# RetNet attention and a PReLU feed-forward layer on one core: a planner that counts changes between kinds of matmul, and a last unit ordered by accumulator

## The chip, the cores and the metric

The kernel runs on one core of a Trainium2 chip. The metric is device time in microseconds (us). The engines are TensorE (PE in the profile; PEld are its weight loads), VectorE (DVE), ScalarE (ACT), GpSimd (POOL) and SyncE (SP), which issues nearly all DMAs. Each engine works through its own queue in order and waits on semaphores for the others.

## The reference

```python
# q, k, v: (8 batches, 8 heads, 576, 64), fp32
scores = 1/sqrt(64) * q @ k^T
Dmat   = where(rel >= 0, gamma[h] ** rel, 0)        # gamma[h] = 1 - 2**(-5-h)
x      = ((scores * Dmat) @ v)  -> (4608 tokens, 512)
h      = x @ w_in                                   # 512 x 2048
g      = max(h, 0) + alpha * min(h, 0)
out    = g @ w_out                                  # 2048 x 512
```

## The kernel before, in words

**The feed-forward layer** is cut into 18 blocks of 256 tokens and 8 units of 256 hidden columns. A *cell* is one block with one unit. A *visit* is one block with several units in a row (`order`): first 17 visits with units 0 to 3, then one with all eight, then 17 visits with units 4 to 7. The four PSUM banks `pso` gather a visit's output and are emptied after its last cell (`evacuate`, L1116): one operation takes in the second accumulator `p1` (VectorE at L1123, or a ScalarE copy at L1127 in first visits), a second one on VectorE combines it with the first accumulator `p0` (L1128), and a DMA writes the result. This is done for each half `m` of the block's tokens.

**Products of pieces.** Plain fp32 products on TensorE are slow. So every operand is split into pieces in a type with fewer mantissa bits (`fp32r`), and three products of pieces replace one fp32 product: two go into one accumulator, and the product of the *differences* (piece 2 of each operand) goes into another. `unit` (L1042) does so for `x @ w_in`: 12 matmuls for each half `f` of the unit's columns (L1057) into the bank `psh[f]`, then two ScalarE and two VectorE operations for each (the last is L1071, and it frees the bank). `split_g` makes the pieces of g on ScalarE and GpSimd. `second` (L1093) does `g @ w_out`: for each m six matmuls at L1105, two cells later (`LAG`). The first 8 cells are done in plain fp32 (`unit_plain` L992, `second_plain` L1023) while the weights are being read and split.

**Attention.** Heads go in 32 pairs. The first eight pairs (batches 0 and 1) are done in the first 110 us by other routines, in fp32. For the other 24, `joint(n)` (L840) gives TensorE three groups of small fp32 matmuls (`GROUPS`): `v0` and `v1`, the values of the pair before (L808, 36 matmuls in two halves, into `psh[0]` and `psh[1]`), and `x` with `su`, the scores and the state sums of this pair (L860, L867, L870, into `psh[1]` and two banks `psa`). The masks (L888) and the state recurrence (L902) follow on VectorE. I call one `joint` an attention step. The banks `psh` are shared with `unit`, so a step's first half must wait for the unit's L1071.

**What sets the order.** The kernel lists operations with `do(engine, cost, function, reads, writes, ...)` and then calls `plan()` (L238). A first pass, backwards, gives each operation a due time. A second pass builds each engine's queue: among the operations whose inputs are done it takes the earliest possible start `t0`, keeps those that could start within `SLACK` after it (0.14 us on TensorE, 0.05 elsewhere), and of these picks the one with the earliest due time. An operation whose `kind` is not that of the one before it on its engine counts as later by `SWITCH` (0.12 on TensorE). The kind is the engine, save for the group with `su`, whose kind is `"half"`. TensorE may run ahead in the program by up to 150 operations. The chip then runs the queues in this order: planned times are no times on the chip, only the order is.

```python
return t + SWITCH.get(op.eng, 0.0) * (kinds[op.eng] != op.kind)
...
t, op = min((x for x in c if x[0] <= t0 + SLACK.get(e, 0.05)),
            key=lambda x: (due[x[1].n], x[1].n))
```

Of the kernel before, what the change touches and what calls it, by code (L numbers as in the profile page):

```python
# [21 lines left out]
def kernel(  # L22
# [315 lines left out]
    BACKLOG, HOLD = 2.0, 30.0  # L338
    LAG, HOLD_X = 2, 100.0
    GROUPS = (("v0",), ("v1",), ("x", "su"))  # L340
    SLACK, SWITCH = {"PE": 0.14}, {"PE": 0.12}
    BEGIN = {"PE": 5.0, "ACT": 0.5, "DVE": 8.2, "POOL": 5.8, "SP": 0.5}


# [488 lines left out]
    def on_pe(parts, groups):  # L833
        for some in groups:
            do("PE", sum(parts[x][0] for x in some), lambda some=some: [parts[x][1]() for x in some],
               [key for x in some for key in parts[x][2]],
               [key for x in some for key in parts[x][3]],
               kind="half" if "su" in some else None)

    def joint(n):  # L840
        pv = [Gen(psh[m]) for m in range(2)]
        parts = {}
        if n - 1 in mts:
            (parts["v0"], parts["v1"]), rest = values(n - 1, pv)
        if n == len(pairs):
            on_pe(parts, [["v0"], ["v1"]])
            rest()
            return
        c = pairs[n][1]
        kT, qT = turned[n]  # L850
        kn, vn = loaded[n][2:]

        ss, uu = (Gen(x) for x in psa)

        def chunks(x):
            return x.get().rearrange("p (j s) -> p j s", s=C)

        def f():
            for h2 in range(2):
                nc.tensor.matmul(pv[1].get()[half(h2), 7 * C:], kT.get()[half(h2), chunk(NJ - 1)],  # L860
                                 qT.get()[half(h2), chunk(NJ - 1)], start=True, stop=True)
        parts["x"] = 0.067, f, [(kT, 0), (qT, 0)], [(pv[1], "x")]

        def f():
            for j in range(NJ - 1):
                for h2 in range(2):
                    nc.tensor.matmul(chunks(ss)[half(h2), j], kT.get()[half(h2), chunk(j)],  # L867
                                     qT.get()[half(h2), chunk(j)], start=True, stop=True,
                                     skip_group_check=True)
                    nc.tensor.matmul(chunks(uu)[half(h2), j], kn.get()[half(1 - h2), j],  # L870
                                     vns[n % 2][half(1 - h2), h2, j], start=True, stop=True,
                                     skip_group_check=True)
        parts["su"] = (1.05, f, [(kT, 0), (qT, 0), (kn, 0), (kn, 1), (vn, "v", 0), (vn, "v", 1)],
                       [(ss, 0), (uu, 0), (uu, 1)])
        on_pe(parts, [some for some in ([x for x in group if x in parts] for group in GROUPS)
                      if some])
        if n - 1 in mts:
            rest()
            if n + 1 < len(pairs):
                load_v(n + 1)  # L880
        mt = mts[n] = Gen(ats)
        for h2 in range(2):
            to = lambda h2=h2: mt.get()[half(h2), h2].rearrange("p j s -> p (j s)")
            dma(to, lambda h2=h2: qT.get()[half(h2)], S * D * 4, [(qT, 0)], [(mt, "q", h2)])

        def masked(h2, j, fro):
            x, h = half(h2), 2 * c + h2
            nc.vector.scalar_tensor_tensor(  # L888
                out=mt.get()[half(1 - h2), h2, j], in0=fro[x], scalar=pf[x, 1, h:h + 1],
                in1=mask[x, None, :].to_broadcast([C, fro.shape[1], C]), op0=ALU.mult,  # L890
                op1=ALU.mult)
        for h2 in range(2):
            do("DVE", 0.69, lambda h2=h2: masked(h2, slice(0, NJ - 1), chunks(ss)), [(ss, 0)],
               [(mt, "s", h2)])
        for h2 in range(2):
            do("DVE", 0.285, lambda h2=h2: masked(h2, slice(NJ - 1, NJ), chunks(pv[1])[:, 7:]),
               [(pv[1], "x")], [(mt, "x", h2)])
        su = Gen(sus)
        g1, g2 = gch[:, 0, c:c + 1], gch[:, 1, c:c + 1]
        do("ACT", 0.37, lambda: nc.scalar.copy(su.get()[:, 0::2], chunks(uu)[:, 0::2]), [(uu, 0)],  # L900
           [(su, "e")])
        do("DVE", 0.45, lambda: nc.vector.scalar_tensor_tensor(  # L902
            out=chunks(uu)[:, 1::2], in0=su.get()[:, 0::2], scalar=g1, in1=chunks(uu)[:, 1::2],
            op0=ALU.mult, op1=ALU.add), [(su, "e")], [(uu, 1)])
        do("ACT", 0.22, lambda: nc.scalar.copy(su.get()[:, 1], chunks(uu)[:, 1]), [(uu, 1)],
           [(su, 1)])
        for j in range(3, NJ - 1, 2):
            do("DVE", 0.285, lambda j=j: nc.vector.scalar_tensor_tensor(
                out=su.get()[:, j], in0=su.get()[:, j - 2], scalar=g2, in1=chunks(uu)[:, j],
                op0=ALU.mult, op1=ALU.add), [(su, j - 2), (uu, 1)], [(su, j)])  # L910
        do("DVE", 0.42, lambda: nc.vector.scalar_tensor_tensor(
            out=su.get()[:, 2::2], in0=su.get()[:, 1:NJ - 3:2], scalar=g1,
            in1=chunks(uu)[:, 2::2], op0=ALU.mult, op1=ALU.add),
            [(su, 1), (su, 3), (su, 5), (uu, 0)], [(su, "e")])
        for h2 in range(2):
            to = lambda h2=h2: vns[n % 2][half(h2), h2, 1:]
            keys = [(su, x) for x in ("e", 1, 3, 5, 7)]
            dma(to, lambda h2=h2: su.get()[half(h2)], (S - C) * D * 4, keys, [(vn, "s", h2)])
# [123 lines left out]
    def unit(cell):  # L1042
        vis, u = cell["vis"], cell["u"]
        x = vis["x"]
        ga = Gen(gas[cell["n"] % 2])
        for f in range(2):
            ph = Gen(psh[f])

            def at(b, ph=ph):
                return ph.get()[:, b * TB:(b + 1) * TB]  # L1050

            def mm(f=f, at=at):
                for n, (b, l) in enumerate(((0, 0), (1, 2), (0, 1))):
                    for cc in range(NCC):
                        w = w_piece(u, cc // 2, l)
                        c0 = (cc % 2 * 2 + f) * P
                        nc.tensor.matmul(at(b), w[:, c0:c0 + P],  # L1057
                                         piece(x.get()[:, l, cc]), start=(n == 0 and cc == 0),
                                         stop=(n > 0 and cc == NCC - 1), skip_group_check=True)
            do("PE", 1.43, mm, [(x, l, n) for l in range(3) for n in range(2)] +  # L1060
               [w_at[u, i][l] for i in range(2) for l in range(3)], [(ph, 0), (ph, 1)])
            fc = 2 * u + f
            g = lambda f=f: ga.get()[:, f]
            do("ACT", 0.36, lambda g=g, at=at: nc.scalar.copy(g(), at(1)), [(ph, 1)], [(ga, f)])  # L1064
            do("DVE", 0.42, lambda g=g, at=at: nc.vector.scalar_tensor_tensor(  # L1065
                out=g(), in0=at(0), scalar=ONE, in1=g(), op0=ALU.mult, op1=ALU.subtract),
                [(ph, 0)], [(ga, f)])
            do("ACT", 0.39, lambda g=g, at=at: nc.scalar.activation(at(1), g(), ACTF.Relu,  # L1068
                                                                    scale=-1.0),
               [(ga, f)], [(ph, 1)])  # L1070
            do("DVE", 0.48, lambda g=g, at=at, fc=fc: nc.vector.scalar_tensor_tensor(  # L1071
                out=g(), in0=at(1), scalar=malpha[:, fc:fc + 1], in1=g(), op0=ALU.mult,
                op1=ALU.add), [(ph, 1), (cst, "a")], [(ga, f)])
        cell["ga"] = ga
# [18 lines left out]
    def second(cell):  # L1093
# [5 lines left out]
                dma(lambda: vis["o"].get(), lambda: o_kept[vis["kb"]], P * 4096,  # L1099
                    [(okm[vis["kb"]], 0), (okm[vis["kb"]], 1)], [(vis["o"], 0), (vis["o"], 1)])  # L1100
        for m in range(2):
            def mm(m=m, a=list(acc)):
                for f in range(2):
                    for b, l in ((0, 0), (0, 1), (1, 2)):
                        nc.tensor.matmul(a[2 * m + b].get(),  # L1105
                                         piece(g.get()[:, l, f, m * P:(m + 1) * P]),
                                         w_piece(u, 2 + f, l),
                                         start=(cell["first"] and f == 0 and l != 1),
                                         stop=(cell["last"] and f == 1 and l > 0))
            do("PE", 1.375, mm, [(g, l) for l in range(3)] +  # L1110
               [w_at[u, i][l] for i in (2, 3) for l in range(3)],
               [(acc[2 * m], 0), (acc[2 * m + 1], 0)])
            if cell["last"]:
                evacuate(vis, m)

# [248 lines left out]
```

## Time and profile before

| | |
|---|---|
| Median of three runs | 954.3 us (952.51 to 955.4) |
| The profiled execution, its own time | 958.57 us |
| Its span, first to last instruction | 956.5 us |
| Mean granted TensorE clock | 0.994 of full |
| TensorE busy | 930.8 us, 97% of the span |
| VectorE, ScalarE, GpSimd busy | 554.1, 573.8, 576.8 us |
| L1057 / L1105, share of the chain that ended last | 40% / 39% |

The span is what the profiler recorded between the first and the last instruction; the execution's own time has some 2 us more around it. A matmul's shown duration contains its way through the array, which overlaps the next one: the difference of two starts is what it costs in a row. "PE psh L808 <- DVE ga L1071" reads: TensorE's instruction of line 808, which writes psh, waited for VectorE's instruction of line 1071.

### The profile page before, as it was taken

To read this page: it belongs to the slowest core of one execution; us is meant where nothing else is said; L and a number is where in the kernel's file an instruction comes from. 1 tells how busy PE (TensorE), PEld (TensorE's weight loads), DVE (VectorE), ACT (ScalarE), POOL (GpSimd) and SP (SyncE) were. 2 spreads that over 40 slices of the span, in tenths; PEclk is the share of its full clock that TensorE was granted. 3 is DMA by queue.
4 is the path that set the end of the run, shared out by engine and by line. 5 is a ranking of instruction groups with operands and counts; after the bars stand their busy time and mean duration, and the time that the engine had idled before them with its cause. 6 is when DMAs were issued, how large, how long until landed. Compare 5 with 4: busy or idle time off the path is not lost.

```text
span 956.5 us, 22974 instructions
## 1 busy us (share of the span) xinstructions
PE 930.8 (97%) x9009; PEld 820.8 (86%) x9009; DVE 554.1 (58%) x1180; ACT 573.8 (60%) x1285; POOL 576.8 (60%) x473
## 2 busy tenths in 40 slices
PE   4899999999999999999999999999999999999998
PEld 4666689888988898888999999999999999999996
DVE  5668566665766676766665754544444554444444
ACT  3446556657667666657876775555555555555542
POOL 3557765748865668745775565555555555555543
PEclk9899999999999999999999999999999999999999
DMA  8867587777877877785434411122222111121212
GB/s 213 203 178 149 134 182 170 151 173 166 186 181 179 199 178 171 209 174 147 155 121 144 156 54 45 67 78 78 86 88 70 67 67 66 66 67 68 66 45 66
DMA packets 235532, 121.05 MB, mean 127 GB/s; under 512 B 203408, under 2 KB 203424, under 8 KB 235424
## 3 DMA queue, kind: packets, MB, share of 16 engines
q1 hardware_dynamic: 233312, 119.05, 47.4%
q8 instruction: 71, 1.16, 0.5%
q10 hardware_dynamic: 2112, 0.53, 0.3%
q14 instruction: 37, 0.30, 0.1%
HBM read 74.19 MB, written 31.98 MB: 111 GB/s over the span
## 4 chain that ended last, share of the span: by engine, by line
PE 91%; DVE 2%; POOL 2%; ACT 2%; issue 1%; DMA 1%; ACTq 0%; POOLq 0%; DVEq 0%
PE psh L1057 40%; PE pso L1105 39%; PE psh L808 3%; PE pso L1023 2%; PE psh L992 2%; PE psa L870 2%; DMA w<-in_q_dram 1%; PE psh L860 1%; PE psa L867 1%; POOL w L732 1%; ACT x L571 1%; DVE psa L679 0%; POOL w L423 0%; ACT w L669 0%; POOL lx L975 0%
## 5 line engine op out<-in xcount | busy, mean ns | idle before, releaser
L1057 PEld LDWEIGHTS psh<-lx,w 128*128 128x128 f32 x2832 | 356.3, 191 | 11.6 <-DVE ga L1071 0.6
L1057 PE MATMUL psh<-lx,w 128*128 128x256 f32 x2832 | 364.2, 284 | 0.0
L1105 PE MATMUL pso<-w,g 128*128 128x512 f32 x1416 | 350.0, 393 | 1.4 <-DVE o L1128 1.2
L1084 POOL TENSOR_TENSOR g<-ga,g 128x512 fp32r<-128x512 f32 x136 | 175.8, 1293 | 243.4 <-ACT g L1080 217.8
L1105 PEld LDWEIGHTS pso<-w,g 128*128 128x128 f32 x1416 | 256.5, 189 | 50.0 <-DVE o L1128 1.4
L1065 DVE SCALAR_TENSOR_TENSOR ga<-psh,ga 128x256 f32<-128x256 f32 x272 | 115.0, 423 | 192.8 <-ACT ga L1064 189.3
L1087 POOL TENSOR_TENSOR g<-g 128x512 fp32r<-128x512 f32 x136 | 176.0, 1294 | 11.7 <-ACT g L1082 1.5
L1064 ACT COPY ga<-psh 128x256 f32<-128x256 f32 x272 | 101.3, 373 | 134.7 <-PE psh L1057 118.4
L1071 DVE SCALAR_TENSOR_TENSOR ga<-psh,malpha,ga 128x256 f32<-128x256 f32 x272 | 130.7, 481 | 69.5 <-ACT psh L1068 68.6
L1068 ACT ACTIVATE psh<-ga 128x256 f32<-128x256 f32 x272 | 105.6, 388 | 82.1 <-DVE ga L1065 81.8
L1080 ACT ACTIVATE g<-ga 128x512 fp32r<-128x512 f32 x136 | 85.7, 630 | 55.9 <-DVE ga L1071 52.1
L975 POOL TENSOR_TENSOR lx<-lx 128x512 fp32r<-128x512 f32 x66 | 84.7, 1295 | 44.4 <-DVE lx L965 36.2
L1082 ACT ACTIVATE g<-ga 128x512 fp32r<-128x512 f32 x136 | 84.4, 620 | 0.0
L888 DVE SCALAR_TENSOR_TENSOR at<-psa,pf,mask 64x512 f32<-64x512 f32 x48 | 36.0, 750 | 31.6 <-PE psa L867 29.0
L958 ACT ACTIVATE lx<-x 128x512 fp32r<-128x512 f32 x66 | 41.2, 627 | 0.0
L808 PEld LDWEIGHTS psh<-at,vn 128*64 128x64 f32 x864 | 27.9, 137 | 10.8 <-issue 6.8
L972 POOL TENSOR_TENSOR lx<-x,lx 128x512 fp32r<-128x512 f32 x24 | 31.0, 1294 | 5.0 <-DVE wa L681 2.1
L693 POOL TENSOR_TENSOR wa<-wa,op 128x512 int32<-128x512 int32 x16 | 21.0, 1311 | 21.5 <-DVE wa L690 11.7
L808 PE MATMUL psh<-at,vn 128*64 128x64 f32 x864 | 32.6, 226 | 1.1 <-DVE ga L1071 1.1
L1123 DVE TENSOR_TENSOR op<-pso,op 128x512 f32<-128x512 f32 x34 | 23.3, 687 | 15.3 <-PE pso L1105 15.3
L965 DVE TENSOR_TENSOR lx<-x,psa 128x512 fp32r<-128x512 f32 x42 | 28.5, 679 | 2.7 <-PE psh L1057 2.1
L827 ACT COPY x<-psh 128x256 f32<-128x256 f32 (+3 forms) x72 | 20.7, 321 | 15.3 <-PE psh L808 11.7
(210 smaller groups left out, 1114.4 us busy)
## 6 DMA issues: line engine op xcount, KB each, us to landing
xk<-x SPq DMA_DIRECT2D x18, 512.0 KB, 4.2
out_dram<-o SPq DMA_DIRECT2D x36, 256.0 KB, 2.3
ok<-o SPq DMA_DIRECT2D x34, 256.0 KB, 3.2
x<-xk SPq DMA_DIRECT2D x17, 512.0 KB, 4.9
op<-ok SPq DMA_DIRECT2D x17, 512.0 KB, 4.0
qx<-in_q_dram SPq DMA_DIRECT2D x96, 72.0 KB, 3.1
kx<-in_k_dram SPq DMA_DIRECT2D x96, 72.0 KB, 2.7
kn<-in_k_dram SPq DMA_DIRECT2D x48, 144.0 KB, 3.2
```

The lines of the kernel that those rows point to most:

```text
L808: nc.tensor.matmul(pv[i].get()[half(h2), (j - js[0]) * C:(j - js[0] + 1) * C], vns[n % 2][:, h2, j], mt.get()[:, h2, j], start=True, stop= ...
L975: do("POOL", 1.29, lambda c=c: nc.gpsimd.tensor_tensor(out=piece(to.get()[:, 2, c]), in0=to.get()[:, 0, c], in1=to.get()[:, 1, c], op=ALU. ...
L1057: nc.tensor.matmul(at(b), w[:, c0:c0 + P], piece(x.get()[:, l, cc]), start=(n == 0 and cc == 0), stop=(n > 0 and cc == NCC - 1), skip_grou ...
L1064: do("ACT", 0.36, lambda g=g, at=at: nc.scalar.copy(g(), at(1)), [(ph, 1)], [(ga, f)])
L1065: do("DVE", 0.42, lambda g=g, at=at: nc.vector.scalar_tensor_tensor(out=g(), in0=at(0), scalar=ONE, in1=g(), op0=ALU.mult, op1=ALU.subtrac ...
L1068: do("ACT", 0.39, lambda g=g, at=at: nc.scalar.activation(at(1), g(), ACTF.Relu, scale=-1.0), [(ga, f)], [(ph, 1)])
L1071: do("DVE", 0.48, lambda g=g, at=at, fc=fc: nc.vector.scalar_tensor_tensor(out=g(), in0=at(1), scalar=malpha[:, fc:fc + 1], in1=g(), op0=A ...
L1080: do("ACT", 0.64, lambda: nc.scalar.mul(piece(to.get()[:, 2]), ga.get(), BELOW), both, [(to, 2)])
L1082: do("ACT", 0.64, lambda: nc.scalar.mul(piece(to.get()[:, 0]), ga.get(), BELOW * 2.0 ** -12), both, [(to, 0)])
L1084: do("POOL", 1.29, lambda: nc.gpsimd.tensor_tensor(out=piece(to.get()[:, 1]), in0=ga.get(), in1=to.get()[:, 2], op=ALU.subtract), both + [ ...
L1087: do("POOL", 1.29, lambda: nc.gpsimd.tensor_tensor(out=piece(to.get()[:, 2]), in0=to.get()[:, 0], in1=to.get()[:, 1], op=ALU.subtract), [( ...
L1105: nc.tensor.matmul(a[2 * m + b].get(), piece(g.get()[:, l, f, m * P:(m + 1) * P]), w_piece(u, 2 + f, l), start=(cell["first"] and f == 0 a ...
```

## The change

Four edits to what the planner is told, and one to the order of matmuls:

- the width `SLACK` of TensorE's choice goes from 0.14 to 0.3, and the price `SWITCH` from 0.12 to 0.1;
- the kinds are drawn anew: products of pieces (`unit`, `second`) have the kind `"pieces"`, all other TensorE work keeps the kind of the engine, and the group with `su` is no longer a kind of its own;
- some costs that the planner reads change: `x` 0.067 to 0.02, `su` 1.05 to 1.09, the masks 0.69 to 0.75, the first step of the recurrence 0.45 to 0.485;
- in a visit's last cell, `second` becomes two operations for each m: first the two products of differences (term `(1, 2)`, into accumulator `2m + 1`), then the other four (into `2m`). In all other cells the six stay one operation in the order of before.

```diff
-    SLACK, SWITCH = {"PE": 0.14}, {"PE": 0.12}
+    SLACK, SWITCH = {"PE": 0.3}, {"PE": 0.1}
...
             do("PE", sum(parts[x][0] for x in some), lambda some=some: [parts[x][1]() for x in some],
                [key for x in some for key in parts[x][2]],
-               [key for x in some for key in parts[x][3]],
-               kind="half" if "su" in some else None)
+               [key for x in some for key in parts[x][3]])
...
-        parts["x"] = 0.067, f, [(kT, 0), (qT, 0)], [(pv[1], "x")]
+        parts["x"] = 0.02, f, [(kT, 0), (qT, 0)], [(pv[1], "x")]
...
-        parts["su"] = (1.05, f, [(kT, 0), (qT, 0), (kn, 0), (kn, 1), (vn, "v", 0), (vn, "v", 1)],
+        parts["su"] = (1.09, f, [(kT, 0), (qT, 0), (kn, 0), (kn, 1), (vn, "v", 0), (vn, "v", 1)],
...
-            do("DVE", 0.69, lambda h2=h2: masked(h2, slice(0, NJ - 1), chunks(ss)), [(ss, 0)],
+            do("DVE", 0.75, lambda h2=h2: masked(h2, slice(0, NJ - 1), chunks(ss)), [(ss, 0)],
...
-        do("DVE", 0.45, lambda: nc.vector.scalar_tensor_tensor(
+        do("DVE", 0.485, lambda: nc.vector.scalar_tensor_tensor(
...
             do("PE", 1.43, mm, [(x, l, n) for l in range(3) for n in range(2)] +
-               [w_at[u, i][l] for i in range(2) for l in range(3)], [(ph, 0), (ph, 1)])
+               [w_at[u, i][l] for i in range(2) for l in range(3)], [(ph, 0), (ph, 1)], kind="pieces")
...
         for m in range(2):
-            def mm(m=m, a=list(acc)):
-                for f in range(2):
-                    for b, l in ((0, 0), (0, 1), (1, 2)):
-                        nc.tensor.matmul(a[2 * m + b].get(),
-                                         piece(g.get()[:, l, f, m * P:(m + 1) * P]),
-                                         w_piece(u, 2 + f, l),
-                                         start=(cell["first"] and f == 0 and l != 1),
-                                         stop=(cell["last"] and f == 1 and l > 0))
-            do("PE", 1.375, mm, [(g, l) for l in range(3)] +
-               [w_at[u, i][l] for i in (2, 3) for l in range(3)],
-               [(acc[2 * m], 0), (acc[2 * m + 1], 0)])
+
+            terms = ((0, 0), (0, 1)), ((1, 2),)
+            for some in reversed(terms) if cell["last"] else (sum(terms, ()),):
+                def mm(m=m, a=list(acc), some=some):
+                    for f in range(2):
+                        for b, l in some:
+                            nc.tensor.matmul(a[2 * m + b].get(),
+                                             piece(g.get()[:, l, f, m * P:(m + 1) * P]),
+                                             w_piece(u, 2 + f, l),
+                                             start=(cell["first"] and f == 0 and l != 1),
+                                             stop=(cell["last"] and f == 1 and l > 0))
+                do("PE", 0.459 * len(some), mm, [(g, l) for _, l in some] +
+                   [w_at[u, i][l] for i in (2, 3) for _, l in some],
+                   [(acc[2 * m + b], 0) for b in sorted({b for b, _ in some})], kind="pieces")
             if cell["last"]:
                 evacuate(vis, m)
```

## The prediction

> **What bounds the kernel now.** I read the page's engine table first, then the stages by window, then who kept TensorE waiting, then TensorE's order of instructions around the attention steps, and last the end of the chain of waits.
>
> The engine table:
>
> ```profile
> PE 930.8 (97%) x9009; PEld 820.8 (86%) x9009; DVE 554.1 (58%) x1180; ACT 573.8 (60%) x1285; POOL 576.8 (60%) x473
> ```
>
> No other engine is above 60%, so the order and the kind of TensorE's matmuls set the time. The stages (length, then busy time and instructions of each engine, granted clock, DMA share, GB/s):
>
> ```profile
> 24.00:110.00 86.00, 79.49 (x1295) 56.92 (x1295) 56.64 (x97) 46.03 (x86) 53.73 (x48) 0.97 0.72 170
> 110.00:455.00 345.00, 342.45 (x4245) 301.19 (x4244) 229.10 (x513) 222.34 (x532) 226.01 (x181) 1.00 0.74 174
> 455.00:945.00 490.00, 490.00 (x3138) 446.98 (x3137) 252.18 (x514) 296.73 (x656) 285.12 (x222) 1.00 0.25 83
> ```
>
> From 455 to 945 us TensorE never stops, and only products of pieces run there: no order of the same matmuls is shorter. From 110 to 455 us the attention steps (fp32 matmuls on 64 rows or columns) are mixed into the products of pieces, with 2.55 us of idle time. From 24 to 110 us all is fp32, with 6.5 us of idle time. TensorE's waits after 110 us (who, for whom: us in total, times, longest):
>
> ```profile
> PE pso L1105 <- DVE o L1128: 1.2, 1, 1.2
> PE psh L808 <- DVE ga L1071: 1.1, 3, 0.6
> PE pso L1105 <- POOL g L1087: 0.3, 1, 0.3
> ```
>
> How the kinds follow each other, on TensorE's timeline: first a stretch of pieces alone, then an attention step cut in two, then one in one piece. (Starts are exact; shown lengths overlap, so a duration is the difference of starts.)
>
> ```profile
> 606.54 2.91 PE L1105 MATMUL pso<-w,g 128*128 128x512 f32 x12
> 609.29 0.40 PE L1057 MATMUL psh<-lx,kx 128*128 128x256 f32 x2
> ...
> 612.16 2.91 PE L1105 MATMUL pso<-w,g 128*128 128x512 f32 x12
> ```
>
> ```profile
> 174.49 1.55 PE L1105 MATMUL pso<-w,g 128*128 128x512 f32 x6
> 175.97 0.80 PE L808 MATMUL psh<-at,vn 128*64 128x64 f32 x20
> 176.70 1.66 PE L1105 MATMUL pso<-w,g 128*128 128x512 f32 x6
> 178.29 0.69 PE L808 MATMUL psh<-at,vn 128*64 128x64 f32 x16
> ...
> 180.10 1.70 PE L1057 MATMUL psh<-lx,w 128*128 128x256 f32 x12
> ```
>
> ```profile
> 392.02 1.27 PE L808 MATMUL psh<-at,vn 128*64 128x64 f32 x36
> ...
> 394.42 2.29 PE L1057 MATMUL psh<-lx,w 128*128 128x256 f32 x17
> ```
>
> Alone, twelve L1105 matmuls take 609.29 - 606.54 = 2.75, so six take 1.375. Six before an attention part take 175.97 - 174.49 = 1.48 (0.105 more); six between two parts take 178.29 - 176.70 = 1.59 (0.215 more). And the attention work itself, 36 of L808 and then scores and state sums, takes 2.40 in one piece (392.02 to 394.42) but 0.73 + 1.81 = 2.54 in two. One cut costs 1.48 + 1.59 + 2.54 = 5.61 against 1.375 + 1.48 + 2.40 = 5.255: **0.355 us a cut**. I counted the cuts along this timeline from 110 to 455 us: nine of the 24 steps are cut (at 133, 176, 190, 218, 235, 291, 361, 376 and 437 us).
>
> The end of the chain (start, us, what):
>
> ```profile
> 944.84 5.91 PE pso L1105 x26
> ...
> 950.77 0.70 DVE op L1123
> ...
> 951.49 0.69 DVE o L1128
> 952.18 0.64 DVE op L1123
> ...
> 952.85 0.69 DVE o L1128
> ```
>
> The last matmul ends at 952.09; then two VectorE operations of 0.69 follow, one after the other, and the output's transfer.
>
> **What the Trainium skill says.** "TensorEngine Tiling (Array Packing)", Key Properties: changing the tiling mode, not just the tile, drains TensorE. The trace agrees: L808 works on 64 columns, L1105 on 128, and each border costs about 0.1 us. "TensorE: Matmul & The Clock Gate", Part 2, step 1: only weight loads are pulled ahead, matmuls stay in program order. The trace agrees: in the one wait of 1.17 us (412.58) no later matmul steps in, so an order planned a little wrong is paid in full. "PSUM — Partial Sum Buffer", Terms: two engines must not be in one bank (and quadrant) at once. The kernel before does as this says: each VectorE read of an accumulator starts after that bank's last product. Products sorted by bank therefore let one bank be read while the other is being filled.
>
> **The change part by part.** Against the profiled execution's own time, 958.57 us (its span is 956.5).
>
> *Last unit's products by bank.* For each visit the two matmuls into the second accumulator come first, then the four into the first one. The same six matmuls (1.375), no extra weight load, no DMA moved. In the middle of the run the subtraction or copy starts four matmuls earlier, 4 x 2.75 / 12 = 0.92, and nothing waits there except once at 412 us. At the end it shows: the first half's subtraction then runs under TensorE; its second operation goes at 950.77; the second half's subtraction follows at about 951.5, its bank being full at 950.74 + 0.46 = 951.2; and the last operation starts at about 952.2 instead of 952.85. Gain 0.65 to 0.71; I take **-0.7**. If the planner orders the last four groups otherwise it is 0: bounds 0 and -0.7.
>
> *Changes of kind counted at 0.1 between pieces and everything else.* Before, 0.12 was counted only around the group of scores and sums, even between it and the L808 work beside it, where the trace shows no cost, and nothing was counted where the 0.1 is really lost. Now, after the first L808 half, a piece product counts as 0.1 later, and with the width of 0.3 the second half is still a candidate when it is ready up to 0.4 later (0.14 before). So I ask when the second half could have started: its bank is free at the end of the L1071 operation of the unit's second half, plus 0.06 (133.35 to 133.41 in the trace). The waits against the end of the first half: 176 us 0.27, 190 us none, 218 us none, 291 us 0.06, 361 us 0.17; at 376 us 0.71 and at 133 us 1.36, too late; 235 and 437 us are of another pattern. Five cuts fall: 5 x 0.355 - 0.27 - 0.06 - 0.17 = 1.28. I take **-1.3**. Bounds: all nine fall without idle time, 9 x 0.355 = -3.2; or the earlier due time, which still decides inside the width, keeps them cut, 0.
>
> *The waits.* 0.31 + 0.27 us at 133 us belong to a cut step, 0.18 and 0.62 to the last two steps, 1.17 to the evacuation at 412 us. A new order moves them all; the two at 133 us are the likeliest to go if that step starts one group later: **-0.6**; bounds -2.55 (all gone) and +1.5 (two more like the largest of before).
>
> *Width 0.3 instead of 0.14.* The planner may leave TensorE idle up to 0.3 for an operation with an earlier due time. At 0.14 the trace shows no such idle time except the five waits, so such near misses are rare. Leaving pieces for an attention part now tolerates 0.3 - 0.1 = 0.2 instead of 0.14: 24 steps x 0.06 = 1.4 at most; among pieces 0.3 instead of 0.14. I take **+0.4**; bounds 0 and +5 (an idle of 0.2 in each of the 24 steps). Between 24 and 110 us all is one kind, so only the width acts: waits of 6.5 us can be shuffled; I take 0, bounds -1.5 and +1.5, a wait like the largest there (1.7) lost or gained.
>
> *Other costs.* 0.69 to 0.75 for the masks (the trace has 750 ns), 0.45 to 0.485 (0.49), 0.067 + 1.05 to 0.02 + 1.09: numbers that only the planner reads, the last pair nearly the same sum. Nothing on the chip, 0; their effect on order lies within the bounds above. Where a gap closes in an attention step the next limit is TensorE's own matmuls.
>
> Sum: -0.7 - 1.3 - 0.6 + 0.4 = **-2.2**, so 956.4 for the profiled execution, 0.23%; on the median of 954.3 this is **952.1**.
>
> **The rivals.** *Nearly all cuts and waits go:* of 3.2 + 2.55 + 0.7 = 6.45 us some 4.5 is gained, 949.8. For it: two cuts fall without idle time and two with next to none. Against it: two lack 0.7 us or more. *Only the end is gained:* the due time decides inside a width three times the price of a change, so the cuts stay, -0.7: 953.6. For it: before, the due time also decided. Against it: a second half that is ready anyway has the earlier due time by its place in the program. *TensorE waits for what is due (the other side):* the wider choice puts idle time before the first L808 part of the steps, where it waits for L1071 and the bank. It costs up to 0.2 each against pieces and 0.3 among them; at 0.25 in each of 24 steps, +6.0 against a gain of 2.6, it is +3.4: 957.7. It decides from about 0.11 us a step on against any gain, and from 0.23 for a slowdown that can be told. Against it: TensorE is at 342.45 of 345 us in this stage with the width of 0.14.
>
> **How the numbers follow.** Main case 0.50, nearly all 0.24, only the end 0.15, waiting 0.11. 0.3% is 2.86 us (the three runs shown spread by as much): faster is under 951.44, slower over 957.16. The main case, with a spread of about 1.5, is under 951.44 in a third, which with 0.95 of the second gives 0.40; slower comes from two thirds of the last, 0.08; same 0.52. The range goes from 948.5 (most of the second case) to 956.2 (all but the waiting case and its early variant).
>
> **What would show it.** Right: fewer L808 groups than steps-plus-nine on TensorE's timeline, six L1105 at 1.59 nearly gone, the last subtraction before TensorE's last end, the stage 455 to 945 us unchanged in length. Wrong: idle time before L808 or L1057 in most steps, or new waits before 110 us; a difference of more than 2 us before 110 us would mean that the width, not the counting, decides the result.

## The result

The changed kernel takes 949.32 us (median) against 954.3 before: the ratio is 0.994, with a 95% interval of 0.9922 to 0.9959. That is 5.0 us or 0.52% by the medians, inside the range and beyond the forecast of 952.1, close to the rival in which nearly all cuts and waits go (949.8). Run a second time beside other kernels it gave 0.9953 (0.9939 to 0.9968).

The engine table of the changed kernel, the line that answers to the first one shown of before:

```profile
PE 924.4 (98%) x9009; PEld 817.5 (86%) x9009; DVE 549.3 (58%) x1180; ACT 572.0 (60%) x1285; POOL 576.6 (61%) x473
```

The same 9009 matmuls, 6.4 us less of busy time. To see where, I cut both traces at three points that mean the same work in both: the first matmul of the first attention step, the first matmul after the last L808 and the end of the last matmul. First the kernel before (length, then busy time and instructions of each engine, clock, DMA share, GB/s):

```profile
0.00:112.19 112.19, 93.46 (x1605) 68.03 (x1605) 71.07 (x154) 54.75 (x99) 65.24 (x72) 0.95 0.73 176
112.19:451.66 339.47, 336.92 (x4214) 296.99 (x4213) 226.53 (x508) 218.66 (x524) 220.56 (x176) 1.00 0.75 176
451.66:952.09 500.43, 500.43 (x3196) 455.81 (x3192) 255.06 (x518) 300.40 (x663) 290.95 (x227) 1.00 0.25 82
```

Then the changed kernel:

```profile
0.00:107.59 107.59, 90.08 (x1606) 65.09 (x1606) 70.15 (x154) 54.73 (x99) 65.25 (x72) 1.00 0.78 183
107.59:442.16 334.57, 333.94 (x4214) 296.57 (x4213) 225.36 (x507) 216.20 (x524) 220.85 (x176) 1.00 0.77 179
442.16:942.52 500.36, 500.36 (x3192) 455.83 (x3192) 253.07 (x520) 301.08 (x663) 290.48 (x226) 1.00 0.25 82
```

- *The start* is 4.60 us shorter, and this is no effect of the change. The traces of the two kernels show the same instructions in the same order on every engine in the first 106 us, and the clock granted in the profiled execution of before was 0.95 of full speed there, against 1.00. In the profiles below the start takes 106.5 to 112.3 us, and the two kernels change places: with the changed kernel's order it took 112.27 us in the run with nine cuts put in, with the order of before 107.10 in the run with six cuts taken out.
- *The stage with the attention steps* is 4.89 us shorter for the same work (1152 matmuls of `unit`, 552 of `second`, 864 values, 1632 scores and state sums and 12 in plain fp32 for the feed-forward layer, by a count along both timelines). From here on "the stage" is this one.
- *Pieces alone* take 0.07 less: nothing.
- *The end*, from the last matmul to the last VectorE operation's end, takes 0.75 in place of 1.46 us; the last transfer then took 0.40 longer in this execution.

So -4.60 - 4.89 - 0.07 - 0.71 + 0.40 = -9.87, the difference of the spans (956.53 and 946.65). What belongs to the change, the stage, the pieces alone and the end, is 5.67 us or 0.59%, as the ratio of 0.994 has it; the stage is most of it.

TensorE's waits from 110 us on (who, for whom, us in total, times, longest) in the changed kernel:

```profile
PE psh L808 <- DVE ga L1070: 0.5, 1, 0.5
```

Before there were five, 2.55 us. A wait costs more than this list says, because the shown length of a matmul reaches past the point where the next one could have started. The longest wait of before shows it on TensorE's timeline:

```profile
410.78 0.64 PE L1057 MATMUL psh<-lx,w 128*128 128x256 f32 x4
412.58 2.11 PE L1105 MATMUL pso<-w,g 128*128 128x512 f32 x8 [1.17 <-DVE o L1128]
```

Four L1057 at 0.12 us from start to start reach to 411.26, so the next product started 1.32 late, not 1.17. The eight L1105 show 2.11 where 2.01 is usual (1.55 for six, and twice 0.229): the second product after the wait lost another 0.10. Counted like this for every wait, by how much later than usual the next matmul starts and, among products of pieces, the one after it, the waits of before cost 3.49 us in the stage and those of the changed kernel 0.78. I call this the *waits in full*.

On TensorE's timeline the step shown in two parts at 174 us now stands in one piece:

```profile
169.28 1.55 PE L1107 MATMUL pso<-w,g 128*128 128x512 f32 x6
170.76 1.31 PE L808 MATMUL psh<-at,vn 128*64 128x64 f32 x36
...
173.19 0.50 PE L1056 MATMUL psh<-lx,w 128*128 128x256 f32 x2
```

Four steps are still cut (at 129, 211, 230 and 256 us), where nine were; TensorE changes between pieces and fp32 57 times in the stage, where it was 67. And the chain at the end (start, us, what) has one VectorE operation after the last matmul:

```profile
936.85 5.68 PE pso L1107 x25
942.53 0.05 issue
942.58 0.69 DVE o L1130
```

### The profile page after: what moved, and what is told of

Read it like the earlier page. It is cut to its first block, busy times and chain, and to the rows that moved or that the text cites. A ratio compares the mean times of both kernels' runs of the same rounds, so it can differ in the third digit from the quotient of the medians.

```text
span 946.7 us, 22947 instructions
## 1 busy us (share of the span) xinstructions
PE 924.4 (98%) x9009; PEld 817.5 (86%) x9009; DVE 549.3 (58%) x1180; ACT 572.0 (60%) x1285; POOL 576.6 (61%) x473
## 4 chain that ended last, share of the span: by engine, by line
PE 92%; DMA 3%; ACT 2%; SPq 1%; DVE 1%; issue 0%; POOL 0%; ACTq 0%; DVEq 0%
PE psh L1056 41%; PE pso L1107 39%; PE psh L808 3%; PE pso L1022 3%; PE psh L991 2%; PE psa L869 2%; SPq L220 1%; ACT x L571 1%; DMA w<-in_q_dram 1%; PE psh L859 1%; PE psa L866 1%; DMA lx<-in_moe_w_out_dram 0%; DMA w<-in_k_dram 0%; DMA lx<-in_moe_w_in_dram 0%; DMA w<-in_moe_w_in_dram 0%
## 5 line engine op out<-in xcount | busy, mean ns | idle before, releaser
L808 PEld LDWEIGHTS psh<-at,vn 128*64 128x64 f32 x864 | 27.5, 138 | 8.9 <-issue 6.4
L780 POOL TENSOR_TENSOR qx<-qx,tabx 128x576 f32<-128x576 f32 x24 | 27.5, 1147 | 12.1 <-DVE wa L690 7.6
L808 PE MATMUL psh<-at,vn 128*64 128x64 f32 x864 | 31.4, 225 | 0.5 <-DVE ga L1070 0.5
L1056 PE MATMUL psh<-lx,kT 128*128 128x256 f32 x144 | 29.0, 283 | 0.0
L869 PE MATMUL psa<-vn,kn 64*64 64x64 f32 x768 | 28.5, 223 | 0.0
```

What stands on the lines that cost most here:

```text
L808: nc.tensor.matmul(pv[i].get()[half(h2), (j - js[0]) * C:(j - js[0] + 1) * C], vns[n % 2][:, h2, j], mt.get()[:, h2, j], start=True, stop= ...
L1056: nc.tensor.matmul(at(b), w[:, c0:c0 + P], piece(x.get()[:, l, cc]), start=(n == 0 and cc == 0), stop=(n > 0 and cc == NCC - 1), skip_grou ...
```

## The experiments

Since the start varies by 6 us between executions, the stage's length is the sharper measure; it came out as 334.57 and 334.55 in two profiles of the changed kernel. The table has it for all runs, with TensorE's idle time in it (length less busy time), the waits in full and the changes of kind, counted along the timeline. The ratio is of the whole kernel, start included, over several runs; the stage is from one profile. The two agree within 2 us: for kinds alone the ratio gives 1.0 us where the stage has 2.3, for kinds and width 6.3 where it has 4.5.

| kernel | stage | idle | waits in full | changes | ratio to before (95%) |
|---|---|---|---|---|---|
| before | 339.47 | 2.55 | 3.49 | 67 | |
| changed | 334.57 | 0.63 | 0.78 | 57 | 0.9940 (0.9922 to 0.9959) |
| changed, again | 334.55 | 0.64 | 0.78 | 57 | 0.9953 (0.9939 to 0.9968) |
| kinds alone | 337.15 | 2.03 | 2.79 | 59 | 0.9989 (0.9978 to 1.0000) |
| width alone | 335.45 | 0.57 | 0.92 | 61 | 0.9950 (0.9932 to 0.9968) |
| last unit alone | 337.41 | 1.58 | 2.34 | 63 | 0.9975 (0.9959 to 0.9991) |
| costs alone | 341.80 | 3.43 | 4.04 | 77 | 1.0034 (1.0021 to 1.0047) |
| kinds and width | 335.02 | 1.33 | 1.81 | 53 | 0.9934 (0.9919 to 0.9949) |
| changed, width 0.22 | 336.88 | 0.90 | 1.05 | 67 | 0.9963 (0.9948 to 0.9978) |
| changed, 0.22 and 0.14 | 334.38 | 0.57 | 0.92 | 55 | 0.9941 (0.9923 to 0.9959) |
| changed, nine cuts put in | 337.80 | 0.52 | 0.59 | 75 | 0.9983 (0.9968 to 0.9997) |
| before, six cuts taken out | 339.24 | 3.65 | 5.42 | 55 | 1.0007 (0.9988 to 1.0025) |
| before, last unit's matmuls reordered | 339.44 | 2.55 | 3.48 | 67 | 1.0005 (0.9993 to 1.0017) |
| kinds, width, matmuls reordered | 334.30 | 0.69 | 1.09 | 53 | 0.9943 (0.9927 to 0.9960) |

Theory A: the gain is the changes of kind and the waits together. Rivals: the counting of kinds makes it (B), any edit deals the order anew by chance (C), the earlier evacuation of a bank takes the waits away (D).

### The price of a cut

The changed kernel with its order kept on every engine, save that the first half of the values is moved ahead of the products of pieces before it wherever that was possible (nine steps); `steps` holds the TensorE operations of each attention step:

```diff
     best = plan()
+    line = best[1]
+    for tag in steps:
+        if "v0" in tag:
+            pe = [op for op in line if op.eng == "PE"]
+            n = pe.index(tag["v0"])
+            if pe[n + 1] is tag["v1"] and pe[n - 1].kind == pe[n - 2].kind == "pieces":
+                op, at = tag["v0"], {o: i for i, o in enumerate(line)}
+                if max([at[d] for d in op.deps]) < at[pe[n - 1]] and pe[n - 1].cost < 1.4 and pe[n - 1].cost > 1.3:
+                    line.remove(op)
+                    line.insert(at[pe[n - 1]], op)
```

> The changed kernel, its planned order kept, but in nine attention steps that were in one piece the first half of the values is moved ahead of the six products of pieces before it: nine cuts more (18 changes of kind), so more changes than the kernel before has. The prediction's price: 9 x 0.355 = +3.2 us, stage 337.8 in place of 334.57, if the first half is ready by then (it stands where the kernel before has it). With waits of up to 0.3 at each for the bank: up to +5.7. If changes of kind cost next to nothing and the waits made the whole gain: below +1.

The stage of this kernel:

```profile
112.27:450.07 337.80, 337.28 (x4214) 296.60 (x4213) 225.65 (x507) 215.69 (x523) 220.93 (x176) 1.00 0.75 177
```

337.80 - 334.57 = 3.23 us for nine cuts, 0.359 each; the prediction had 0.355 from one pair of timelines. No wait was added; a stop of 0.12 us at the stage's end went, so the price is a little low rather than high. The changes of kind have a price of their own, 0.18 each, almost twice the 0.1 that the planner counts; 0.14 of the 0.36 a cut is that the values take more in two parts than in one.

### Cuts taken out by hand

The kernel before, where in six steps the products between the two halves are moved ahead of the first half, all other queues as planned (in a seventh, at 235 us, six of the eighteen products between the halves are moved, and the cut stays):

```diff
     best = plan()
+    line = best[1]
+    for tag in steps:
+        if "v0" in tag:
+            at = {op: n for n, op in enumerate(line)}
+            first, then = sorted((tag["v0"], tag["v1"]), key=lambda op: at[op])
+            for op in [op for op in line[at[first] + 1:at[then]] if op.eng == "PE"]:
...
+                    line.remove(op)
+                    line.insert(at[first], op)
```

> The kernel before, its planned order kept, but in six attention steps the six products of pieces that stand between the two halves of the values are moved ahead of the first half: six cuts fewer (12 changes of kind), and the queues of all other engines exactly as planned. The prediction's price: 6 x 0.355 = -2.1 us, stage from first scores to last values 337.3 in place of 339.46. If only the number of changes counts, that is all. Rival (a cut can't be taken out by itself: the values start 1.4 us later than the other engines' queues were laid out for, so what stands behind their evacuation on ScalarE and VectorE comes late and TensorE waits for it): waits of TensorE at these six places grow by more than the 2.1 gained, +2 to +5 us, stage 341 to 344.

The stage, and TensorE's waits in it:

```profile
107.10:446.34 339.24, 335.59 (x4214) 296.53 (x4213) 226.25 (x508) 217.35 (x524) 220.65 (x176) 1.00 0.76 177
```

```profile
PE pso L1109 <- DVE o L1132: 1.2, 1, 1.2
PE psh L808 <- DVE ga L1075: 1.1, 3, 0.6
PE pso L1109 <- POOL g L1091: 0.5, 2, 0.3
PE psh L1061 <- ACT x L827: 0.5, 1, 0.5
PE psh L1061 <- DVE at L892: 0.4, 1, 0.4
```

Six cuts should give 6 x 0.359 = 2.15 us; the stage gave 0.23. Idle time grew by 1.10: part of the second POOL wait and the two last lines are new. They are at places that were moved (the one for L827 at the seventh): a unit after values waits for its bank, which ScalarE (L827, the values' evacuation) or VectorE (L892, the masks) frees later, since the values came 1.4 us later than these queues were laid out for. In full the waits grew by 5.42 - 3.49 = 1.93 us, and 2.15 less 1.93 is the 0.2 that was measured. The rival holds in its mechanism, not in its size (+2 to +5): cuts pay if the planner takes them out and lays out the other queues to match.

### Each part of the change alone

Only the kinds and the price:

```diff
-    SLACK, SWITCH = {"PE": 0.14}, {"PE": 0.12}
+    SLACK, SWITCH = {"PE": 0.14}, {"PE": 0.1}
...
-               [key for x in some for key in parts[x][3]],
-               kind="half" if "su" in some else None)
+               [key for x in some for key in parts[x][3]])
...
-               [w_at[u, i][l] for i in range(2) for l in range(3)], [(ph, 0), (ph, 1)])
+               [w_at[u, i][l] for i in range(2) for l in range(3)], [(ph, 0), (ph, 1)], kind="pieces")
...
-                [(acc[2 * m], 0), (acc[2 * m + 1], 0)])
+                [(acc[2 * m], 0), (acc[2 * m + 1], 0)], kind="pieces")
```

> Only the kinds and the price of 0.1 of the change; width 0.14, costs and last unit as before. Its planned order has 58 changes of kind on TensorE after 112 us where the kernel before has 66. Theory A (changes of kind and waits both count, 0.18 us a change): 8 x 0.18 = 1.4 less, but its plan still holds waits of 1 to 1.8 us at about 130, 168 and 411 us, some 0.8 more than before: -0.6 us, 0.999 of before. Rival B (the counting of kinds makes the gain): at least half of the 5.0 us, -2.5 or better. Rival C (any edit of the planner's numbers deals the order anew, by chance): anything from -4 to +4, unrelated to the number of changes.

Only the width:

```diff
-    SLACK, SWITCH = {"PE": 0.14}, {"PE": 0.12}
+    SLACK, SWITCH = {"PE": 0.3}, {"PE": 0.12}
```

> Only the width 0.3; kinds, price, costs and last unit as before. Planned order: 60 changes of kind, planned waits about 1.9 us fewer than before. Theory A: 6 x 0.18 + 1.9 = -3.0 us, 0.997. Rival B (the counting makes the gain): 0, within 1 us. The prediction's term for the width (+0.4, TensorE left idle for what is due): slower by 0 to 1 us.

Only the last unit (the last hunk of the change, without the kinds):

```diff
-            def mm(m=m, a=list(acc)):
...
+            terms = ((0, 0), (0, 1)), ((1, 2),)
+            for some in reversed(terms) if cell["last"] else (sum(terms, ()),):
+                def mm(m=m, a=list(acc), some=some):
...
```

> Only the last unit's products of differences first; planner's numbers as before. The end: last matmul to last VectorE operation 0.75 us in place of 1.45, -0.7 in all theories. Beyond that the planner's order changes too: 62 changes of kind, waits 0.8 fewer: theory A -0.7 - 0.7 - 0.8 = -2.2 us, 0.998. Rival D (the earlier evacuation frees banks and takes most waits away): -3 or better, and the wait of TensorE for the evacuation at about 412 us gone. If only the end counts: -0.7.

Only the four costs:

```diff
-        parts["x"] = 0.067, f, [(kT, 0), (qT, 0)], [(pv[1], "x")]
+        parts["x"] = 0.02, f, [(kT, 0), (qT, 0)], [(pv[1], "x")]
...
-            do("DVE", 0.69, lambda h2=h2: masked(h2, slice(0, NJ - 1), chunks(ss)), [(ss, 0)],
+            do("DVE", 0.75, lambda h2=h2: masked(h2, slice(0, NJ - 1), chunks(ss)), [(ss, 0)],
...
```

> Only the four costs that the planner reads (scores, state sums, masks, first step of the recurrence); all else as before. The prediction gave them 0 and left their effect on the order within its bounds. Planned order: 76 changes of kind in place of 66, and about 4 us more of waits. Theory A: 10 x 0.18 + 4 = +5.6 us, 1.006. Rival B: 0. Rival C (dealt anew by chance): also far from 0, but without a tie to the changes and waits planned.

The stages of these four, in this order:

```profile
111.80:448.95 337.15, 335.12 (x4213) 296.89 (x4212) 225.44 (x507) 218.83 (x524) 222.23 (x177) 1.00 0.77 178
107.15:442.60 335.45, 334.88 (x4214) 296.40 (x4213) 226.55 (x507) 218.14 (x524) 222.57 (x177) 1.00 0.77 179
107.49:444.90 337.41, 335.83 (x4213) 296.62 (x4213) 225.65 (x507) 217.93 (x524) 221.92 (x177) 1.00 0.76 177
107.42:449.22 341.80, 338.37 (x4214) 297.84 (x4213) 226.43 (x505) 217.13 (x523) 221.61 (x177) 1.00 0.74 175
```

Width alone gives -4.02, four fifths of the stage's gain, with the old kinds, which speaks against B. It took all waits after 131 us away, and six changes. Kinds alone take away eight changes and leave 2.03 us of idle time (-2.32, more than theory A's -0.6, since the planned waits came out shorter). The last unit alone has -2.06 in the stage beside the 0.7 at the end. The costs, of which those of the masks and of the recurrence are nearer to the trace than before (it has 0.75 and 0.49 us), make it 2.33 *longer* alone: ten changes more, and 0.88 more of idle time, at other places:

```profile
PE psh L1057 <- ACT x L827: 1.9, 3, 1.1
PE psh L808 <- DVE ga L1071: 1.4, 2, 0.9
```

The parts don't add up: -2.32 - 4.02 - 2.06 + 2.33 = -6.07 in the stage against the -4.89 of all together. Every edit deals the order anew (C), but the result is not without a tie to the plan: the changes that were planned came out in each run, to one, and in the table the stages follow the changes and the waits, as the next section shows.

### Counting and waiting taken apart

The changed kernel with the width 0.22 has as many changes as the kernel before, and few waits:

```diff
-    SLACK, SWITCH = {"PE": 0.3}, {"PE": 0.1}
+    SLACK, SWITCH = {"PE": 0.22}, {"PE": 0.1}
```

> The changed kernel with the width 0.22 and the price of 0.1 kept: its planned order has 66 changes of kind, as many as the kernel before (the changed kernel has 56), but planned waits of 1 us less than the changed kernel's and 3.7 less than before. Theory A: changes 0, waits about -2.2 (2.55 were seen before, little can be left), end -0.7: about -3 us against before, some 2 us short of the changed kernel in changes but 0.5 better in waits. Rival B (fewer changes make the gain): only the end, -0.7. Rival W (the waits make all of it): as fast as the changed kernel or faster, -5.

Its stage:

```profile
107.64:444.52 336.88, 335.98 (x4214) 296.71 (x4213) 227.47 (x508) 217.79 (x525) 220.78 (x176) 1.00 0.76 178
```

Against before: no change of kind less, -2.59 us, of which 1.65 is idle time. Against the changed kernel: ten changes more, +2.31, of which 5 x 0.359 = 1.80 is cuts and 0.27 idle time. In full the waits fell by 3.49 - 1.05 = 2.44 us against before, so with the changes equal they make nearly the whole difference. This is theory A, and neither of the two alone.

The whole table bears it out. Take 0.18 us a change, from the run with nine cuts put in, and the waits in full, and count from the changed kernel: 334.57 + 0.18 x (changes - 57) + (waits - 0.78). This gives every stage of the table within 0.4 us, those of single parts and those reordered by hand too. For the kernel before it is 339.08 of 339.47, with six cuts taken out 338.85 of 339.24.

Kinds and width together, without costs and last unit (both diffs above, with a price of 0.1):

> Kinds, price 0.1 and width 0.3 together, without the four costs and without the last unit's order: 52 changes of kind (66 before), planned waits 1.7 us shorter than before. Theory A: -14 x 0.18 - 1.7 = -4.2 us; the end unchanged at 1.45 us between the last matmul and the last VectorE operation. Rival D (the last unit's order is what gives the gain): above -1. If the parts add up as they were alone (stage -2.3 for the kinds, -4.0 for the width): -6.3.

-4.45 in the stage with 53 changes, 0.43 more than the width alone; the end stays at 1.45 us. So neither the costs nor the last unit's two operations are needed for the stage's gain.

### The last unit's order by itself

Before, with its planned order untouched; only the six matmuls inside a last unit's group are sorted by bank:

```diff
-                for f in range(2):
-                    for b, l in ((0, 0), (0, 1), (1, 2)):
+                six = [(f, b, l) for f in range(2) for b, l in ((0, 0), (0, 1), (1, 2))]
+                for f, b, l in sorted(six, key=lambda x: -x[1]) if cell["last"] else six:
```

> The kernel before with its planned order untouched on every engine; only inside each last unit's group of six matmuls the two products of differences come first. The end: from the last matmul to the last VectorE operation 0.76 in place of 1.46 us, -0.7. The stage from first scores to last values: 339.46 as before, but for the wait for the evacuation at about 412 us (1.17), which would shrink if the bank is freed earlier; I expect it to stay, since ScalarE reached that evacuation 5 us late by its own queue. Rival D (bank freed earlier takes waits away): stage below 338.5.

The end of its chain:

```profile
944.99 4.32 PE pso L1105 x19
949.31 0.42 issue
949.73 0.69 DVE o L1128
```

One VectorE operation is left after the last matmul, as expected, but in this execution 0.42 us passed between the two, for which the profile names no cause, so the end took 1.12 in place of 0.76. In the stage nothing moved (339.44), and the wait of 1.17 us for the evacuation is still there: against D. With the same edit on kinds and width:

> Kinds, price 0.1 and width 0.3 on the kernel before, with the order of matmuls inside each last unit's group as in the run before this one, so without the costs and without two operations for the planner. Theory A: the order of the run with kinds and width (948.1, stage 335.0) with 0.7 less at the end: about 947.4 and stage 335.0. If the last unit's own operations are needed for the gain: no faster than 948.1.

Here the end took 0.76, and the stage fell from 335.02 to 334.30 with the same order on all engines. Two waits shrank: 0.20 us at 130 us is gone, and of 0.47 us for ScalarE's L827 at 259 us only 0.03 is left. The first comes before the reordering can act, since the first accumulator that it touches is emptied at 146 us; ScalarE waited for a transfer there, 1.20 and 0.69 us. The second goes back to L669 in ScalarE's queue, which waited for a transfer too; first the run with kinds and width, then this one:

```profile
256.57 0.68 ACT L669 ACTIVATE wa<-op 128x512 f32<-128x512 f32 x1 [1.61 <-DMA op<-in_moe_w_in_dram]
260.17 0.68 ACT L669 ACTIVATE wa<-op 128x512 f32<-128x512 f32 x1 [1.17 <-DMA op<-in_moe_w_in_dram]
```

The transfer took 5.2 us from issue to landing in the one execution and 4.8 in the other, which is most of the difference, and the evacuation (L1126) follows L669 without idle time in both. So the 0.7 us are no sign of the earlier evacuation. D finds no support in either order, and the landing of transfers moves the stage by some tenths between executions of one order.

### A search for a better pair

The changed kernel with a width and a price that give the planner fewer changes and waits:

```diff
-    SLACK, SWITCH = {"PE": 0.3}, {"PE": 0.1}
+    SLACK, SWITCH = {"PE": 0.22}, {"PE": 0.14}
```

> The changed kernel with the price 0.14 and the width 0.22 in place of 0.1 and 0.3: 54 changes of kind in the planned order (the changed kernel has 56, the one before 66), and planned waits 0.9 us shorter than the changed kernel's. Theory A (0.18 a change, and the waits): 2 x 0.18 + 0.9 = 1.2 us less than the changed kernel, about 948.0 where the kernel before has 954.2; the stage from the first scores to the last values about 333.3 us (339.46 before, 334.57 changed). Rival C (the order is dealt by chance and a plan says nothing of the chip): no better than the changed kernel.

> The changed kernel once more, beside the others on one chip. All theories: 0.994 of before, and a profile whose stage from the first scores to the last values is 334.6 us within 0.3, since TensorE is never short of clock there; the first 107 us may differ by up to 5 us between executions.

-0.2 us in the stage in place of the 1.2 expected: two changes fewer are worth 0.36, but the waits that the plan had shorter came out longer, 0.92 in full in place of 0.78. The ratios 0.9941 and 0.9953 can't be told apart. The same holds for kinds and width with and without the sorted matmuls (0.9943, 0.9934). With 0.9 us of waits and some 55 changes left there is little more in this knob: 24 steps need 48 changes even if none is cut.

## Why the prediction was right or wrong

- **The end, -0.7: right.** 1.46 to 0.75 us, in all profiles with the change's last-unit operations.
- **The price of a cut, 0.355: right** (0.359 over nine cuts). **Five cuts fall: right in number** (nine to four), not in name. Of the five that I named, 176, 190, 291 and 361 us fell and 218 us stays (at 211 us, the start being 4.6 us shorter); 376 us, called too late, and 437 us fell too, and one at 256 us is new. The idle time of 0.5 us that I charged did not come: at 171 us the whole step follows at once on the six products of pieces. The cuts gave 5 x 0.359 = 1.80, not 1.3. That the counting made them fall is not shown: kinds alone took eight changes away, the width alone six.
- **The waits, -0.6: the term that was mis-sized.** They gave 3.49 - 0.78 = 2.71 in full; with the cuts' 1.80 this leaves 0.38 of the stage's 4.89 open. Even the bound of -2.55, "all gone", was too small, since it took the listed idle time for the cost. I had named only the two waits at 133 us, and one of these stayed (0.52); the three that I left in place, at 412, 436 and 451 us, are those that went.
- **The width, +0.4: the wrong sign.** Alone it shortened the stage by 4.02. I took it as leave to idle; idle time fell from 2.55 to 0.57. I read "no idle time at 0.14" as a sign that nothing was to be gained from a wider choice. My reading now is that a narrow choice also takes what could start at once over what is due sooner, and pays later where the other engines are late; that the earlier due time is what removed each wait was not tested one by one.
- **The start, 0: right as to the change**, with a difference of 4.6 us in the profiles that belongs to the execution. I had named more than 2 us there as a sign that the width decides and not the counting. The sign came up for another reason; that the width does have the larger part is known from the run with the width alone, and the sign agrees with it by luck.
- **The costs, 0: right within the whole** (kinds, width and sorted matmuls without them have a stage of 334.30), wrong alone (+2.33).
- **"No cost" between values and scores: misread**, without harm. From start to start, 16 values and the border to the scores take 0.62 (178.29 to 178.91), 36 and that border 1.20 (392.02 to 393.22). So a value takes 0.029 and the border adds 0.16; 20 values and a border to products, at 0.029 and 0.16, come to 0.74, and the trace has 0.73. Both borders cost the same, but a step has the one between values and scores whether it is cut or not.

The forecast's -2.2 was less than half of what the stage and the end gave, 5.6. The end and the price of a cut were sound; the waits and the width, which made the larger part, were not, and only the breadth of the range took this in. The new kinds, which were to give most (-1.3), add 0.43 us to what the width gives alone. The forecast's second case, a quarter of the chance, had the right size: 1.8 of 3.2 us in cuts, 2.7 in waits where it allowed 2.55, and 0.7 at the end.

## What to carry to other kernels

Where a planner writes the queues and one engine is full, price two things from the trace: what a change between kinds of work costs on that engine, and what the waits cost in full, from start to start; counted from the changed kernel, the two together come within 0.4 us of each stage of 340 us here. With the listed idle time in place of the waits in full up to 2.0 us stay open. Take a cut out through the planner, not by hand in one queue: six cuts worth 2.15 us gave 0.2 when the other engines' queues stayed as they were, since the waits grew by 1.9. And measure a change of 0.5% on a stage that holds the same work in both traces: here the start alone varied by 6 us between executions of the same work, and by 5 with the same order of all queues (107.10 and 112.19).

## What the runs showed of the hardware

- Going from products of pieces to the small fp32 matmuls, or back, costs TensorE 0.18 us a change, and this contains the 0.14 us that values in two parts take more than in one (nine cuts put in by hand: 3.23 us for 18 changes).
- A wait costs TensorE more than the idle time that its trace shows: 1.42 us for one of 1.17, 3.49 for the five of before that show 2.55.
- Plain fp32 products take longer than the three products of pieces in their place: `second` of one cell took 3.44 us in plain fp32 (eight matmuls in the trace, at 118.24 us of before) and takes 2.75 in pieces (twelve).
- With the same instructions in the same order, the start took 112.19 us where the clock granted in it was 0.95 of full speed, and 107.10 where it was 1.00 (before, and before with six cuts taken out); 112.27 at 0.94 and 107.59 at 1.00 (changed with nine cuts put in, and changed).
